# An attention and MoE kernel: sums' rows ahead of loads on the queue, ScalarE's exponentials ahead of its copies

## The chip, the cores and the metric

The kernel runs on one core of a Trainium2 chip. The core has TensorE (PE, with its weight loads as PEld), VectorE (DVE), ScalarE (ACT), GpSimd (POOL) and SyncE (SP), which here issues every DMA. The metric is the device time of one execution in microseconds (us), taken as the median of several runs.

## The reference

Causal attention over 2 batches of 12 heads, 448 positions, 64 elements per head; its output, laid out as 896 rows of 768, goes through two feed-forward blocks. Everything is float32.

```python
scores = np.where(mask, -1e9, scale * q @ k.T)          # mask: above the diagonal
attn = np.exp(scores - scores.max(-1, keepdims=True))
attn = attn / (attn.sum(-1, keepdims=True) + 1e-09)
x = (attn @ v)                                          # as 896 x 768
h = np.maximum(np.maximum(x @ w1, x @ w2), x @ w3)      # 768 x 768 each
x = h @ w_out
r = np.maximum(x @ w_in, 0.0)                           # 768 x 2048
out = (s * (r * r) + b) @ w_out2                        # 2048 x 768
```

## The kernel before, in words

The first fifth of the time is attention, the rest the feed-forward blocks, whose weights come as 56 tiles (`wraw`) that VectorE and ScalarE decode into a high and a low part. Attention works on 12 pairs of heads in 14 software-pipelined steps. The order of all instructions is the order of the code (`manual_schedule`): in step `s` (`step`, L534) four pairs are in work.

- Pair `s` ("new"): TensorE lays the mask into three PSUM tiles and adds the scores to it: A holds query rows 256 to 383 of both heads, B rows 0 to 255, C the last 64 rows of both heads. Scores are products of a high and a low part (`HL`) of q and k. VectorE takes row minima (`minima`; scores are negated), ScalarE the exponentials (`exps`: index 2 is A, 0 and 1 are B, NQ is C), which also give the row sums `su`, seven numbers for each of 128 partitions.
- Pair `s-1` ("old"): VectorE inverts the sums (`inverses`, L444: add 1e-9, take the reciprocal). TensorE transposes the exponentials in four groups (`transposes`); each group is copied out of one of two PSUM tiles `t` to `PT` (`pt_copy`: groups 0 to 2 by ScalarE, group 3 by VectorE). Between groups 1 and 2 stand the product with V of pair `s-2` and the transpose `st` of the inverted sums (`sums`). `spread` (L456) copies `st` to `rows`, writes `rows` to DRAM (`rcd`) by two DMAs and reads it back by two DMAs as a broadcast `rb`, which have to wait for the write.
- Pair `s-2` ("out"): the product with V (`pv`). It runs over four column blocks j; block j needs the V rows from 128j on.
- Pair `s-3`: `pv_out` (L472) multiplies the product in PSUM by `rb` on VectorE (`xf`), which also frees the one PSUM tile `o` for the next `pv`; GpSimd splits the result for the feed-forward blocks.
- Pair `s+2` ("nxt"): VectorE rounds q and k to the high part (`split_hi`), GpSimd takes the low part (`split_lo`) and copies the last rows into the block-diagonal `bd` (`both_tails`). For pair `s+3` GpSimd scales q (`scaled`).

SP issues in the order of the code and stops at a DMA whose wait has not ended. A DMA also waits for the landing of the eighth one before it, whose semaphore it takes over. At the start of a step stand the load of q and k of pair `s+4` (`R`, 448 KB) and some of the 42 loads of V; the table `V_LOADS` says how many stand there and how many between the write `rcd` and the broadcast `rb`. V comes in four groups: pair 0, pair 1, pairs 2 to 5 (first needed by `pv` in step 4) and pairs 6 to 11 (first needed in step 8). Weight tiles are fetched behind `spread`. Steps 12 and 13 have no new scores; TensorE fills them with the first feed-forward products.

Of the kernel before, what the change touches and what calls it, by code (L numbers as in the profile page):

```python
# [14 lines left out]
ALU = mybir.AluOpType  # L15
# [20 lines left out]
    12: ("hi2", "low3"),  # L36
}
V_GROUPS = ((0, 1), (1, 1), (2, 4), (6, 6))
V_LOADS = ((7, 0), (3, 4), (3, 4), (3, 4), (2, 2), (2, 2), (2, 2), (2, 0))
FILL = {12: (3, 5), 13: (0, 4)}  # L40
WARM = 9
BUSY = (9,)
# [7 lines left out]
def kernel(  # L50
# [39 lines left out]
    def sub_lo(eng, lo, full, hi):  # L90
        eng.tensor_tensor(out=lo, in0=full, in1=hi.bitcast(F32), op=ALU.subtract)  # L91
# [122 lines left out]
    def attention():  # L214
        with ExitStack() as c2:
# [36 lines left out]
            def load(p, cuts=((0, S),)):  # L252
                pair[p]["R"] = R = ld.tile([128, 2, S], F32, tag="R", name="R")
                for a, b in cuts:
                    nc.sync.dma_start(out=R[:, :, a:b], in_=qk[p, :, :, a:b])
# [17 lines left out]
            def load_v(n):  # L273
                for _ in range(min(n, len(v_list))):
                    to, of = v_list.pop(0)
                    nc.sync.dma_start(out=to, in_=of)  # L276
# [13 lines left out]
            def scaled(p):  # L290
                q = pair[p]["R"][:, 0, :]
                pool_scaled(q, q, -scale)
# [4 lines left out]

            def split_lo(p):
                HL, R = pair[p]["HL"], pair[p]["R"]
                sub_lo(nc.gpsimd, HL[:, 1:4:2, :], R, HL[:, 0:4:2, :])  # L300

            def split_hi_early(p):
                new_hl(p)
# [16 lines left out]
            def both_tails(p):  # L320
                HL = pair[p]["HL"].bitcast(F32)
                for h in range(2):
                    pool_scaled(bds[p % 3][hs[h], :, hs[h]], HL[hs[h], 0:2, TAIL:S], 1.0)
# [47 lines left out]
            def minima(p, i):  # L371
                e = pair[p]
                src, cols = (at(p, i), slice(2 * i, 2 * i + 2)) if i < NQ else (e["C"][:, 0:S], slice(2 * NQ, 2 * NQ + 1))
                nc.vector.tensor_reduce(  # L374
                    out=e["mx"][:, cols], in_=src, axis=mybir.AxisListType.X, op=ALU.min
                )
# [14 lines left out]
            def exps(p, i):  # L391
                if i == NQ:
                    exponential(p, pair[p]["C"][:, 0:S], L0, S, 2 * NQ, NQ)
                    return
                for h in range(2):
                    exponential(
                        p, at(p, i)[:, h], p_at(h, i, 0), (i + 1) * TQ, 2 * i + h, h * (NQ + 1) + i
                    )
# [44 lines left out]

            def inverses(p):  # L444
                su = pair[p]["su"]
                nc.vector.tensor_tensor(
                    out=su, in0=su, in1=tiny.to_broadcast([128, 7]), op=ALU.add
                )
                nc.vector.reciprocal(out=su, in_=su)

            def sums(p):
                e = pair[p]
# [81 lines left out]
            def step(s):  # L534
                new, old, out, nxt = (
                    p if 0 <= p < n_pairs else None for p in (s, s - 1, s - 2, s + 2)
                )
                if s + 4 < n_pairs:
                    load(s + 4)
                loads = V_LOADS[s] if s < len(V_LOADS) else (0, 0)  # L540
                load_v(loads[0])
                if new is not None:
                    results(new)
                    if new == 0:
# [21 lines left out]
                if new == 1:  # L566
# [2 lines left out]
                    scores_ab(new, 0)  # L569
                    mask_c(new)  # L570
                    scores_c(new)
                if old is not None:
                    inverses(old)
                if new == 0:
                    for i in (0, 1, 2, NQ):
                        minima(new, i)
                elif new is not None:
                    minima(new, 2)
                if new == 1:
                    split_hi(2)  # L580
                    split_lo(2)
                    both_tails(2)
                    for V in vs[2:]:
                        nc.gpsimd.memset(V[D:128, :, :, NQ, :], 0.0)
                if 0 <= s - 3 < n_pairs - 2:
                    pv_out(s - 3)
                if new:
                    for i in (1, 0, NQ):
                        minima(new, i)
                if old is not None:  # L590
                    pt_copy(old, 0, nc.scalar)
                    pt_copy(old, 1, nc.scalar)
                if new:
                    exps(new, 2)
                if new and s + 3 < n_pairs:
                    scaled(s + 3)
                if new and nxt is not None:
                    split_hi(nxt)
                    split_lo(nxt)
                    both_tails(nxt)  # L600
                if s < len(BUSY):
                    keep_busy(BUSY[s])
                if out is not None:
# [7 lines left out]
                    exps(new, 2)  # L611
                if old is not None:
                    sums(old)
                    spread(old, loads[1])
                    transposes(old, 2)
                    transposes(old, 3)
                for _ in asked + [n for n in FETCH if n == s]:
                    fetch_w()
                asked.clear()
                if old is not None:  # L620
                    pt_copy(old, 2, nc.scalar)
                if new is not None:
                    exps(new, NQ)
                decode(MID.get(s, ()))
                if old is not None:
                    pt_copy(old, 3, nc.vector)
# [197 lines left out]
```

## Time and profile before

| | |
|---|---|
| median of 3 runs | 514.69 us (513.52 to 515.76) |
| the profiled execution's own time | 514.35 us |
| its span from first to last instruction | 512.6 us |
| TensorE busy | 499.0 us, 97% |
| VectorE, ScalarE, GpSimd busy | 348.0, 280.5 and 68.8 us |
| GpSimd's last work | before 110 us of the span |
| DMA bytes moved | 58.34 MB |

The busy shares are means over two stages. Up to about 108 us the attention steps follow each other; all four engines and the queue are in use there, and GpSimd only there. Behind that TensorE works without a gap but the last microseconds. A step can be timed by the mask matmul of tile A (L328), which is the first that TensorE does in it: steps 1 to 11 start at 11.09, 17.27, 23.81, 30.95, 39.79, 46.32, 53.40, 60.78, 71.68, 78.67 and 86.24 us.

### The profile page before, as it was taken

The page shows a single profiled execution, that of the slowest core. Times are in us where ns is not written, and L with a number is a line of the kernel's source. Part 1 is how long each engine was busy: PE and PEld are TensorE (multiplying, and loading weights), DVE is VectorE, ACT ScalarE, POOL GpSimd, SP SyncE. Part 2 cuts the span into 40 slices and gives each one's busy share as a digit, 9 for nine tenths or more (in the row PEclk, how much of TensorE's full clock was granted, in tenths as well). Part 3 has the DMA queues.
Part 4 walks back from the last instruction along what each step waited for, and adds up shares of the span by engine and source line. Part 5 has one row for each costly group of instructions (what it writes and reads, how often), then busy time and mean ns, then how long its engine had stood idle before and what let it go on. Part 6 is the DMA issues. An engine that isn't in the chain of part 4 may idle for free.

```text
span 512.6 us, 7545 instructions
## 1 busy us (share of the span) xinstructions
PE 499.0 (97%) x2910; PEld 454.6 (89%) x2910; DVE 348.0 (68%) x522; ACT 280.5 (55%) x517; POOL 68.8 (13%) x93
## 2 busy tenths in 40 slices
PE   8899979999999999999999999999999999999997
PEld 4767757789999999999999999999999999999997
DVE  4788879558476675758767888888888645384401
ACT  5876757644353453535445787878788333352201
POOL 7876664320000000000000000000000000000000
PEclk9999989999999999999999999999999999999999
DMA  6567631423241332433322332233223333081003
GB/s 197 185 180 213 162 107 38 153 68 123 84 159 66 123 88 98 132 116 124 123 85 101 124 123 82 106 124 123 95 90 124 123 125 123 1 293 61 1 0 109
DMA packets 26068, 58.34 MB, mean 114 GB/s; under 512 B 13532, under 2 KB 17456, under 8 KB 26032
## 3 DMA queue, kind: packets, MB, share of 16 engines
q1 hardware_dynamic: 26032, 57.86, 34.8%
q8 instruction: 23, 0.38, 0.3%
q14 instruction: 13, 0.11, 0.1%
HBM read 55.05 MB, written 2.80 MB: 113 GB/s over the span
## 4 chain that ended last, share of the span: by engine, by line
PE 82%; DMA 7%; DVE 4%; SPq 2%; POOL 2%; ACT 2%; issue 1%; POOLq 0%; DVEq 0%; ACTq 0%
PE m L649 57%; PE m L757 23%; DMA v<-in_v_dram 3%; DMA rcd<-rows 2%; DMA R<-in_qk_dram 1%; PE o L429 1%; SPq L276 1%; POOL HL L91 1%; ACT p L386 1%; DVE mx L374 1%; PE t L413 1%; DVE wa L165 1%; SPq L468 1%; DMA rb<-rcd 1%; PE o L433 1%
## 5 line engine op out<-in xcount | busy, mean ns | idle before, releaser
L649 PE MATMUL m<-x,whi 128*128 128x448 f32 x816 | 232.1, 366 | 1.2 <-ACT wr L146 0.8
L649 PEld LDWEIGHTS m<-x,whi 128*128 128x128 f32 x816 | 152.9, 188 | 13.8 <-ACT wr L146 1.2
L649 PE MATMUL m<-x,wlo 128*128 128x448 f32 x408 | 149.0, 365 | 0.0
L757 PE MATMUL m<-whi,g 128*128 128x384 f32 x448 | 113.9, 334 | 0.0
L183 ACT CAST whi<-wa 128x768 fp32r<-128x768 f32 x56 | 46.8, 835 | 66.5 <-PE m L757 42.3
L649 PEld LDWEIGHTS m<-x,wlo 128*128 128x128 f32 x408 | 76.6, 188 | 6.1
L757 PEld LDWEIGHTS m<-whi,g 128*128 128x128 f32 x448 | 80.8, 188 | 0.0
L143 ACT ACTIVATE wa<-wraw 128x768 f32<-128x768 f32 x56 | 50.9, 910 | 53.7 <-DVE wlo L91 51.2
L91 DVE TENSOR_TENSOR wlo<-wa,whi 128x768 fp32r<-128x768 f32 x56 | 53.5, 956 | 38.9 <-ACT whi L183 38.9
L757 PE MATMUL m<-wlo,g 128*128 128x384 f32 x224 | 74.8, 334 | 0.0
L178 DVE CUSTOM_DVE_ANT_0 wa<-wa,wr 128x1536 uint16<-128x1536 uint16 x56 | 53.6, 957 | 1.9
L171 DVE SCALAR_TENSOR_TENSOR wa<-wraw,wa 128x768 int32<-128x768 int32 x56 | 53.5, 955 | 0.0
L146 ACT ACTIVATE wr<-wraw 128x768 int32<-128x768 uint32 x56 | 50.8, 907 | 0.0
L757 PEld LDWEIGHTS m<-wlo,g 128*128 128x128 f32 x224 | 42.0, 188 | 0.0
L656 DVE TENSOR_TENSOR t<-t,m 128x448 f32<-128x448 f32 x24 | 14.9, 621 | 38.7 <-PE m L649 38.7
L649 PE MATMUL m<-h,whi 128*128 128x448 f32 x144 | 40.9, 365 | 0.0
L165 DVE TENSOR_SCALAR wa<-wa 128x768 int32<-128x768 int32 x56 | 34.2, 610 | 1.8
L419 ACT COPY PT<-t 128x512 f32<-128x512 f32 x36 | 20.2, 597 | 22.1 <-PE t L413 22.1
L742 ACT ACTIVATE r<-m 128x448 f32<-128x448 f32 x32 | 17.5, 546 | 22.1 <-PE m L649 22.1
L429 PE MATMUL o<-PT,v 128*64 128x448 f32 (+3 forms) x96 | 24.8, 401 | 4.8 <-DVE xf L477 4.4
L157 DVE TENSOR_SCALAR wa<-wa 128x768 f32<-128x768 f32 x52 | 28.7, 552 | 0.6 <-ACT wa L143 0.6
L649 PEld LDWEIGHTS m<-h,whi 128*128 128x128 f32 x144 | 27.0, 188 | 2.1
(81 smaller groups left out, 566.1 us busy)
## 6 DMA issues: line engine op xcount, KB each, us to landing
wraw<-in_w_dram SPq DMA_DIRECT2D x56, 768.0 KB, 4.3
R<-in_qk_dram SPq DMA_DIRECT2D x11, 448.0 KB, 5.4
rb<-rcd SPq DMA_DIRECT2D x24, 112.0 KB, 2.7
out_dram<-o SPq DMA_DIRECT2D x14, 192.0 KB, 1.9
v<-in_v_dram SPq DMA_DIRECT2D x4, 96.0 KB
v<-in_v_dram SPq DMA_DIRECT2D x2, 168.0 KB, 6.5
v<-in_v_dram SPq DMA_DIRECT2D x6, 48.0 KB, 2.6
v<-in_v_dram SPq DMA_DIRECT2D x2, 144.0 KB, 4.6
```

Of the source, the lines that this page charges most:

```text
L91: eng.tensor_tensor(out=lo, in0=full, in1=hi.bitcast(F32), op=ALU.subtract)
L143: nc.scalar.activation(out=e["f"], in_=e["high"].bitcast(F32), func=ACTF.Abs)
L146: nc.scalar.activation(out=e["r"], in_=e["low"].bitcast(U32), func=ACTF.Copy, scale=2.0 ** -29)
L157: nc.vector.tensor_scalar(out=e["f"], in0=e["f"], scalar1=UNDER, scalar2=OVER, op0=ALU.max, op1=ALU.min)
L165: nc.vector.tensor_scalar(out=a, in0=a, scalar1=3, scalar2=0x3FFFFFF8, op0=ALU.logical_shift_left, op1=ALU.bitwise_and,)
L171: nc.vector.scalar_tensor_tensor(out=e["a"], in0=e["high"], scalar=-0x40000000, in1=e["a"], op0=ALU.bitwise_and, op1=ALU.bitwise_or,)
L178: nc.vector.tensor_tensor(out=e["a"], in0=e["a"], in1=e["r"], op=ALU.add)
L183: nc.scalar.copy(out=e["hi"], in_=e["f"])
L419: copy(out=pair[p]["PT"][:, n * 512:(n + 1) * 512], in_=pair[p]["t", n])
L429: nc.tensor.matmul(o[hs[0], j * TQ:S], V[:, 0, j], PT[:, at:at + m * TQ + D], **flags)
L649: nc.tensor.matmul(p, wt[w][:, ws], cols(act[i], a, b), start=(i == 0 and n == 0), stop=(i == len(act) - 1 and n == 2),)
L757: nc.tensor.matmul(acc[t][:, 0:EH], gt[f][:, a, ts], w[:, ws], start=(f == 0 and n == 0), stop=(f == KG - 1 and n == 2),)
```

## The change

What it does, in the order of a step:

- The load of q and k of pair `s+4` and the loads of V leave the step's start. `load(s+4)` stands behind `spread`, with V loads behind it; a new `V_LOADS` (first number: between write and broadcast; the others: behind) sets how many.
- `inverses` keeps the reciprocal alone and stands behind the minima of A. The add of 1e-9 is done by ScalarE (`guarded`), right behind the last exponentials of the pair, a step earlier.
- From step 2 on ScalarE takes the exponentials of A ahead of the copies of transpose groups 0 and 1.
- The low parts are taken in two instructions of half the size.
- `scaled(s+3)` stands behind the low parts and tails instead of ahead of them; in step 1 the high and low part of pair 3 stand behind `spread`.

```diff
-V_LOADS = ((7, 0), (3, 4), (3, 4), (3, 4), (2, 2), (2, 2), (2, 2), (2, 0))
+V_LOADS = ((0, 7, 7), (2, 3), (2, 3), (2, 2), (2, 2), (2, 2), (2, 1), (2, 1))
...
-                sub_lo(nc.gpsimd, HL[:, 1:4:2, :], R, HL[:, 0:4:2, :])
+                for n in range(2):
+                    sub_lo(nc.gpsimd, HL[:, 2 * n + 1], R[:, n], HL[:, 2 * n])
...
             def inverses(p):
                 su = pair[p]["su"]
-                nc.vector.tensor_tensor(
-                    out=su, in0=su, in1=tiny.to_broadcast([128, 7]), op=ALU.add
-                )
                 nc.vector.reciprocal(out=su, in_=su)
+
+            def guarded(p):
+                su = pair[p]["su"]
+                nc.scalar.activation(out=su, in_=su, func=ACTF.Identity, bias=tiny)
...
-                if s + 4 < n_pairs:
-                    load(s + 4)
                 loads = V_LOADS[s] if s < len(V_LOADS) else (0, 0)
-                load_v(loads[0])
...
-                if old is not None:
-                    inverses(old)
                 if new == 0:
                     for i in (0, 1, 2, NQ):
                         minima(new, i)
                 elif new is not None:
                     minima(new, 2)
+                if old is not None:
+                    inverses(old)
...
+                if new is not None and new > 1:
+                    exps(new, 2)
                 if old is not None:
                     pt_copy(old, 0, nc.scalar)
                     pt_copy(old, 1, nc.scalar)
-                if new:
+                if new == 1:
                     exps(new, 2)
-                if new and s + 3 < n_pairs:
-                    scaled(s + 3)
-                if new and nxt is not None:
+                if nxt is not None and new > 1:
                     split_hi(nxt)
                     split_lo(nxt)
                     both_tails(nxt)
+                if new is not None and new > 1 and s + 3 < n_pairs:
+                    scaled(s + 3)
...
                     sums(old)
-                    spread(old, loads[1])
+                    spread(old, loads[0])
                     transposes(old, 2)
                     transposes(old, 3)
+                if s + 4 < n_pairs:
+                    load(s + 4)
+                load_v(loads[1])
                 for _ in asked + [n for n in FETCH if n == s]:
                     fetch_w()
                 asked.clear()
+                load_v(sum(loads[2:]))
+                if new == 1:
+                    split_hi(nxt)
+                    split_lo(nxt)
+                    both_tails(nxt)
+                    scaled(s + 3)
...
                 if new is not None:
                     exps(new, NQ)
+                    guarded(new)
```

SP's queue around step 3, before: the load of q and k of pair 7 stands first, the write of pair 2's rows after three V loads, the broadcast last (`v_100` is V of pairs 2 to 5; its 64-row pieces are the last that the product of step 4 needs).

```order
L255 DMA R<-in_qk_dram 128x896
L276 DMA v_100<-in_v_dram 32x4x64
L276 DMA v_100<-in_v_dram 80x4x64 x2
L462 DMA rcd<-rows 7x128
L463 DMA rcd<-rows 1x64
L276 DMA v_100<-in_v_dram 48x4x64 x2
L276 DMA v_100<-in_v_dram 64x4x64 x2
L468 DMA rb<-rcd 64x448 x2
```

The same step on SP's queue, now:

```order
L464 DMA rcd<-rows 7x128
L465 DMA rcd<-rows 1x64
L276 DMA v_100<-in_v_dram 48x4x64 x2
L470 DMA rb<-rcd 64x448 x2
L255 DMA R<-in_qk_dram 128x896
L276 DMA v_100<-in_v_dram 64x4x64 x2
L128 DMA wraw<-in_w_dram 128x768
```

The write and the broadcast now stand first; the load of q and k and the last two pieces of V for step 4 have moved behind the broadcast.

ScalarE in step 2, before (PT is the transposed exponentials, `p` the exponentials of the three score tiles, `su` their sums):

```order
L419 COPY PT<-t 128x512 x2
L386 ACTIVATE p_134,su<-A,mx 128x384 x2
L386 ACTIVATE p_134,su<-B,mx 128x128 x2
L386 ACTIVATE p_134,su<-B,mx 128x256 x2
L419 COPY PT<-t 128x512
L386 ACTIVATE p_134,su<-C,mx 128x448
```

ScalarE in step 2, now:

```order
L387 ACTIVATE p_134,su<-A,mx 128x384 x2
L420 COPY PT<-t 128x512 x2
L387 ACTIVATE p_134,su<-B,mx 128x128 x2
L387 ACTIVATE p_134,su<-B,mx 128x256 x2
L420 COPY PT<-t 128x512
L387 ACTIVATE p_134,su<-C,mx 128x448
L451 ACTIVATE su<-su,tiny 128x7
```

A's exponentials have moved ahead of the two copies, and the add of the constant is new at the end.

VectorE at the start of step 3, before:

```order
L446 TENSOR_TENSOR su<-su,tiny 128x7
L449 RECIPROCAL su<-su 128x7
L374 TENSOR_REDUCE mx<-A 128x2
L477 TENSOR_TENSOR xf<-o,rb 128x448
```

VectorE at the start of step 3, now:

```order
L375 TENSOR_REDUCE mx<-A 128x2
L447 RECIPROCAL su<-su 128x7
L479 TENSOR_TENSOR xf<-o,rb 128x448
```

The minima of A no longer stand behind the inverted sums, and the add has left VectorE.

## Rows read from the trace of the kernel before

**Rows 1.** TensorE's waits: who waited for whom, total us, times, longest.

```profile
PE o L429 <- DVE xf L477: 4.4, 4, 2.8
...
PE t L413 <- DVE rows L461: 1.2, 1, 1.2
...
PE B L336 <- ACT p L386: 0.7, 3, 0.3
```

**Rows 2.** Timeline of TensorE, 30 to 72 us: start, duration, operation [idle before].

```profile
30.95 0.28 PE L328 MATMUL A<-tri,identb 128*128 128x128 bf16 x2
...
39.79 0.28 PE L328 MATMUL A<-tri,identb 128*128 128x128 bf16 x2
...
44.94 0.22 PE L429 MATMUL o<-PT,v 128*64 128x64 f32 x1
...
45.18 0.28 PE L454 MATMUL st<-ident,su 128*7 128x128 f32 x1
...
46.32 0.28 PE L328 MATMUL A<-tri,identb 128*128 128x128 bf16 x2
...
60.78 0.28 PE L328 MATMUL A<-tri,identb 128*128 128x128 bf16 x2
...
67.11 0.59 PE L429 MATMUL o<-PT,v 128*64 128x448 f32 x1 [2.77 <-DVE xf L477]
...
71.68 0.28 PE L328 MATMUL A<-tri,identb 128*128 128x128 bf16 x2
```

**Rows 3.** Stretches: length, busy us (instructions) by engine, PE clock, DMA share, GB/s.

```profile
65.00:67.50 2.50, 0.39 (x2) 0.27 (x4) 1.07 (x2) 1.21 (x5) 0.65 (x3) 1.00 0.97 257
67.50:70.00 2.50, 2.50 (x22) 1.87 (x18) 1.98 (x4) 1.72 (x8) 2.42 (x4) 0.56 0.22 48
...
125.00:150.00 25.00, 25.00 (x125) 23.17 (x124) 17.81 (x27) 11.54 (x16) 0.00 (x0) 1.00 0.38 126
```

**Rows 4.** Chain of waits, 0 to 130 us: start, duration, what.

```profile
35.98 2.37 DMA v<-in_v_dram
```

**Rows 5.** Timeline of SP's queue, 52 to 81 us.

```profile
56.81 0.33 SPq L462 DMA_DIRECT2D rcd<-rows  x1
...
62.89 1.09 SPq L468 DMA_DIRECT2D rb<-rcd  x2
...
64.66 1.30 SPq L276 DMA_DIRECT2D v<-in_v_dram  x2
...
78.14 0.27 SPq L462 DMA_DIRECT2D rcd<-rows  x1
...
79.36 1.09 SPq L468 DMA_DIRECT2D rb<-rcd  x2
```

**Rows 6.** Timeline of VectorE in steps 1, 2, 7, 8 and 10.

```profile
15.67 0.86 DVE L296 CAST HL<-R 128x896 fp32r<-128x896 f32 x1
...
22.98 0.28 DVE L461 COPY rows<-st 7x128 f32<-7x128 f32 x1 [1.50 <-PE st L454]
...
54.93 0.95 DVE L446 TENSOR_TENSOR su<-su,tiny 128x7 f32<-128x7 f32 x1 [0.44 <-ACT p L386]
...
66.43 0.62 DVE L477 TENSOR_TENSOR xf<-o,rb 128x448 f32<-128x448 f32 x1 [3.36 <-DMA rb<-rcd]
...
79.51 1.86 DVE L165 TENSOR_SCALAR wa<-wa 128x768 int32<-128x768 int32 x1
```

**Rows 7.** Groups by line and shape, ScalarE to 92 us: count, busy us, mean ns, idle before.

```profile
L419 ACT COPY PT<-t 128x512 f32<-128x512 f32 x32 | 17.9, 596 | 19.4 <-PE t L413 19.4
```

**Rows 8.** The same for GpSimd to 104 us.

```profile
L91 POOL TENSOR_TENSOR HL<-R,HL 128x896 fp32r<-128x896 f32 x11 | 25.8, 2343 | 2.1 <-DVE HL L296 2.0
L91 POOL TENSOR_TENSOR x<-xf,x 128x448 fp32r<-128x448 f32 x11 | 12.5, 1138 | 0.9
```

**Rows 9.** DMA issues of the page: count, KB each, median us to landing.

```profile
R<-in_qk_dram SPq DMA_DIRECT2D x11, 448.0 KB, 5.4
rb<-rcd SPq DMA_DIRECT2D x24, 112.0 KB, 2.7
```

## The prediction, made before the changed kernel was run

> **What bounds the kernel now.** I read the busy shares by stretch first. Behind attention TensorE is busy for the whole of a stretch at full clock [rows 3], so whatever attention saves or loses there comes through to the end unchanged. The change touches attention alone, and it leaves TensorE's own order as it was. So the question is how much TensorE waits in attention, for whom, and which of these waits goes.
>
> The measure is the length of a step from one mask matmul of A to the next. Step 5 takes 46.32 - 39.79 = 6.53 us [rows 2], and no later step with scores is shorter: I take it as what TensorE needs if nothing keeps it waiting. Step 4 takes 39.79 - 30.95 = 8.84 us, step 8 takes 71.68 - 60.78 = 10.90 us [rows 2]. These two hold most of what can be had: 2.31 and 4.37 us. The rest is in TensorE's list of waits [rows 1]: 4.4 us for `xf` in four waits (2.77 of them in step 8 [rows 2], so 1.6 in the other three), 1.2 us once for `rows` in step 1, and 0.7 us in three waits of the mask of B for ScalarE's exponentials.
>
> Step 8 read from its end: the product with V waits 2.77 us for `xf` [rows 2], which waits 3.36 us for the broadcast `rb` [rows 6]. That broadcast is issued at 62.89, 6.08 us after its write at 56.81 [rows 5]; where nothing else is under way the same distance is 79.36 - 78.14 = 1.22 us [rows 5]. So the write stood behind loads, and SP, which waits for it in order, held up everything behind. Around this wait TensorE is busy 0.39 of 2.50 us, and then the granted clock is 0.56 of full, a mixture of 1.2 and 2.4 GHz [rows 3]. That is where the step's other 4.37 - 2.77 = 1.6 us go.
>
> Step 4 waits for V: the last piece is issued at 35.98 and lands 2.37 us later, on the chain [rows 4]. Of the 2.31 us I put 0.24 down to a mask wait and 2.07 to V.
>
> **The change part by part.**
>
> Write and broadcast ahead of the loads. The 6.08 us shrink towards 1.22 [rows 5], and SP is no longer held for long. Step 8's broadcast then lands in time: from `st` of step 6 to the `xf` that uses it are 46.32 - 45.18 = 1.1 us to the next step [rows 2], one step of 6.53, and in step 8 at least the 2.5 us that step 7 needed to the end of its inverted sums (54.93 + 0.95 - 53.40 [rows 6]), 10.1 in all. The way there is about 0.7 us to the write's issue (0.28 for `st` [rows 2], 0.28 for `rows` [rows 6], the rest between them), 1.2 to the broadcast's, 1.1 for its two issues [rows 5] and 2.7 to landing [rows 9], 5.7 us. Even with the old 6.08 us between write and broadcast it would be 10.6, half a us late. So the whole 4.37 us go, the clock's part included: -4.4.
>
> What the loads pay for it. The load of q and k of one pair moves about one step back. Its landing takes 5.4 us under load [rows 9], its user (`scaled`) stands a step later: hidden, with about 1 us to spare, and nothing if GpSimd waits a little, since the low part is used two steps on. V is another matter. The last pieces for step 4 and for step 8 now stand behind the broadcast and the load of q and k of the step before. From `st` in that step: 0.7 us to the write's issue, 1.22 to the broadcast [rows 5], 64.66 - 62.89 = 1.77 for the two broadcast issues and the load of q and k, 0.65 for the first of two V issues (half of 1.30) [rows 5], then 2.37 from issue to landing [rows 4]: 6.7 us. TensorE needs the last V block one step after `st` less 45.18 - 44.94 = 0.24 us [rows 2], so 6.3 us. At best it waits 0.4 us there. At worst the write is held up as at 56.81, 6.08 instead of 1.22 us [rows 5], and it waits 5.3 us. I am nearer to the first end: what stands ahead of the write in step 3 is one load of q and k (448 KB) and three V pieces (192 KB), and at the 257 GB/s of a full stretch [rows 3] that is 2.5 us, of which some 2 pass while they are being issued. Before, the write at 56.81 had a weight tile of 768 KB on top. So about 0.5 us on the best case: 0.9 us of waiting is left in step 4 instead of 2.07, -1.2; and in step 8, where V comes late too once `xf` is in time, +1.0.
>
> A rule of the Trainium skill speaks against this ordering. The row says 1.22 us from the write of the sums to the broadcast on an empty queue [rows 5]. The page "DMA: Bandwidth & Descriptors", section "Anatomy of one DMA", puts the fixed part of a DMA at about 2.0 us, most of it the receipt of the write, longest towards DRAM. By it (it is fitted to another way of issuing) V would come 0.8 us later in both steps and the sum be 1.6 us worse; the row is from this very pair of DMAs, so I stay with it.
>
> Step 1. `rows` no longer stands behind a rounding of 0.86 us [rows 6] whose place is now after it. Of the 1.2 us that the transposes wait for `rows` [rows 1] I take 0.7, since the minima ahead of it stay: -0.7 (0.4 to 0.9).
>
> Step 2. `scaled(4)` now stands behind pair 3's low part and tails, and the rounding of pair 4 waits for it, with `rows` behind it on VectorE. Price from 0, since VectorE had 1.50 us to spare there [rows 6], to 2.3, the length of the low part [rows 8]. Nearer to the first: +0.3.
>
> ScalarE. It idles 19.4 us over 32 copies, always for the transposes [rows 7]; the exponentials of A can stand in just that gap once their minima are there, so that the exponentials of B end earlier and the next step's mask of B no longer waits: -0.7, all of rows 1. The added operation of 128x7 costs less than a copy of 128x512 (0.596 us [rows 7]) and lies in the same gap: 0. Without that gap it would be up to 12 x 0.6 us of ScalarE, still not TensorE's.
>
> VectorE. The add waited 0.44 us for ScalarE and took 0.95 us in step 7 [rows 6], with the minima of A and `xf` behind it. Both go. That pays in the three smaller waits for `xf`: 1.6 us. In step 10 a decoding operation of 1.86 us stands ahead [rows 6] and stays; I take 0.9 of the 1.6.
>
> Low parts in halves: 2 x 1.138 = 2.28 us instead of 2.343 [rows 8]. GpSimd has slack either way: 0.
>
> The sum: -4.4 - 1.2 + 1.0 - 0.7 + 0.3 - 0.7 - 0.9 = -6.6 us. The profiled execution took 514.35 us, 1.75 more than its span and 0.34 less than the median. So 507.75 for a run like it, and 508.1 as a median.
>
> **The rivals.**
>
> V late, slower. If the write keeps standing behind loads in steps 3 and 7 as at 56.81, V is 5.3 us late in both, and after each of these waits, both longer than the 2.77 us of step 8, the clock falls as it did there for 1.6 us. Against the forecast that is 5.3 - 0.9 = 4.4 in step 4, 5.3 - 1.0 = 4.3 in step 8, and 3.2 for the clock: 508.1 + 11.9 = 520.0. For it: step 4 waits for V already, and these pieces alone lose places on the queue. Against it: no weight tile stands ahead of the write in steps 3 and 7. With the clock falling both times it eats the whole gain from a wait w of 2.7 us in each of the two places (2 x (w - 0.95) + 3.2 = 6.6), and is slower by over 0.5% from 4.0 us (the same sum, 9.2).
>
> V late by half. Waits of 2.9 us in each place, as long as that of step 8, with one fall of the clock: 2.0 + 1.9 + 1.6 = 5.5 on top, 513.6. The same evidence, with the queue half as full.
>
> The broadcast is not earlier enough. It still has to wait for its write, and in step 6 a weight tile, a load of q and k and two V pieces stand ahead of that as before. If `xf` in step 8 still waits half of its 2.77 us and the clock still falls, 1.4 + 1.6 = 3.0 us of the gain stay away: 511.1. A late `xf` covers a late V in step 8, so the 1.0 us there may fall away as well: 510.1. Against it: the 4 us of margin worked out above.
>
> **How the numbers follow.** The forecast, 508.1, has 0.58; the broadcast not early enough (510.1 to 511.1) 0.12; V late by half (513.6) 0.17; V late, slower (520.0) 0.13. A difference of 0.5%, 2.6 us, is about what a measurement of this kernel can tell from no change: 512.1 to 517.3 is the same. So faster 0.70, same 0.17, slower 0.13. The forecast's own range goes from 505.0 (all of the 1.6 us of `xf`, 0.9 in step 1, nothing lost in step 2, V only 0.4 late in both places: 0.7 + 0.2 + 0.3 + 1.1 = 2.3 better, and some more where step 5 is not the floor) to 510.5 (each part at half). To leave out no more than 2 in 10 the range goes up to 513.9, past V late by half.
>
> **What would show it.** Steps 6 to 9 at 6.5 to 6.8 us each; the distance from write to broadcast under 3 us in all steps but 2 and 6, and SP idle between; step 1 at about 5.5; no wait of the mask of B for ScalarE; no half clock near 68 us. Right but mis-sized would be waits of TensorE for V in steps 4 and 8 of 0.4 to 2 us. Wrong would be V waits of 3 us and over with the clock at half behind them, or a new wait of VectorE for GpSimd's `scaled`, which would say that the later loads of q and k and not V set the pace.

## The result, and the profile after

The changed kernel took 519.82 us (median of four: three took 519.51 to 519.84, one took 2466.65), the kernel before 514.37 us beside it: a ratio of 1.0101 with a 95% interval of 1.0072 to 1.013. It is slower by 1%. Run once more on another chip it took 520.72 us against 515.52, a ratio of 1.0116 (1.008 to 1.0152); the profile shown here is of that second run. One caution for the medians and ratios further down: on some chips the stage behind the last product with V takes either 408.4 or 414.0 us in the traces, whichever kernel runs, so that both depend on how many of each were among the runs.

So the kernels are compared by **the length of attention** in their traces, from the first mask matmul of A in step 1 to the last product with V. For the kernel before it is 104.15 - 11.09 = 93.06 us, for the changed kernel 112.51 - 12.26 = 100.25 us, 7.2 us more. Each length is that of one profiled execution; the one kernel that was profiled twice, V early in the next section, gave 87.19 and 87.42 us. (The profiled execution of the changed kernel is the longest of its four, 522.71 us, which adds to the difference.)

TensorE's list of waits in the changed kernel (who waited for whom, total us, times, longest), beside [rows 1]:

```profile
PE o L430 <- DMA v<-in_v_dram: 5.5, 1, 5.5
PE o L439 <- DMA v<-in_v_dram: 4.7, 1, 4.7
...
PE o L430 <- DVE xf L479: 0.7, 1, 0.7
PE t L414 <- DVE rows L463: 0.5, 1, 0.5
PE B L337 <- ACT p L387: 0.3, 1, 0.3
```

What was to go has gone: the waits for `xf` fell from 4.4 us to 0.7, those for `rows` from 1.2 to 0.5, those of the mask of B from 0.7 to 0.3. Two new lines stand above them, and together they are 10.2 us. TensorE's timeline says where (start, duration, operation, idle time before):

```profile
43.69 0.48 PE L430 MATMUL o<-PT,v 128*64 128x64 f32 x2 [5.48 <-DMA v<-in_v_dram]
...
77.95 0.47 PE L439 MATMUL o<-PT,v 128*64 128x64 f32 x2 [4.71 <-DMA v<-in_v_dram]
```

The first is the last block of the product in step 4, which is the first product with V of pairs 2 to 5; the second is the same block in step 8, the first product with V of pairs 6 to 11. Around both the clock fell. Stretches of the changed kernel (length, busy us and instructions of TensorE, its weight loads, VectorE, ScalarE and GpSimd, granted clock, DMA share, GB/s):

```profile
38.21:42.98 4.77, 0.00 (x0) 0.00 (x0) 0.00 (x0) 0.00 (x0) 3.70 (x5) 1.00 0.70 183
42.98:49.81 6.83, 6.12 (x37) 5.42 (x38) 3.33 (x7) 2.82 (x7) 0.56 (x1) 0.50 0.72 204
...
77.11:83.94 6.83, 5.99 (x35) 5.29 (x36) 3.86 (x8) 2.08 (x6) 0.60 (x2) 0.50 0.11 37
```

And the one such stretch of the kernel before, behind the wait of 2.77 us in step 8 [rows 2, 3]:

```profile
67.90:71.31 3.41, 3.41 (x26) 2.90 (x23) 2.25 (x5) 1.72 (x8) 3.41 (x3) 0.51 0.19 55
```

0.50 is the lower of the two levels, 1.2 of 2.4 GHz. Eight transposes take 1.71 us at 44.67, within such a stretch, and 0.87 us at 50.45, behind it; so I count half of the busy time as lost: 6.12 / 2 = 3.1 us and 5.99 / 2 = 3.0 us after the change, 3.41 / 2 = 1.7 us before it.

The steps, each from its first mask matmul to that of the next (us; step 11 to the last product with V), with those of the first repaired version of the next section:

| step | 1 | 2 | 3 | 4 | 5 | 6 | 7 | 8 | 9 | 10 | rest |
|---|---|---|---|---|---|---|---|---|---|---|---|
| before | 6.18 | 6.54 | 7.14 | 8.84 | 6.53 | 7.08 | 7.38 | 10.90 | 6.99 | 7.57 | 17.91 |
| changed | 5.40 | 7.03 | 6.53 | 14.95 | 8.14 | 6.54 | 6.54 | 12.84 | 8.18 | 6.71 | 17.39 |
| V early | 5.40 | 7.01 | 6.54 | 7.63 | 6.54 | 8.04 | 6.54 | 8.33 | 7.08 | 6.70 | 17.38 |

Steps 4 and 5 lose 7.7 us together and steps 8 and 9 lose 3.1; all others together gain 3.7. Steps 4 and 5 stand 23.09 - 2 x 6.53 = 10.0 us over the floor: 5.5 of waiting for V, 0.7 for `xf`, 3.1 for the clock, and 0.8 not put down to anything. Steps 8 and 9 stand 8.0 us over it: 4.7, 3.0 and 0.3.

Why V is late there is read from SP's queue. Its timeline through steps 2 and 3 (start, time spent issuing, line, transfer, count):

```profile
23.39 0.48 SPq L128 DMA_DIRECT2D wraw<-in_w_dram  x1
24.16 0.28 SPq L464 DMA_DIRECT2D rcd<-rows  x1
...
30.15 2.01 SPq L470 DMA_DIRECT2D rb<-rcd  x2
32.25 0.58 SPq L255 DMA_DIRECT2D R<-in_qk_dram  x1
32.88 1.41 SPq L276 DMA_DIRECT2D v<-in_v_dram  x3
34.39 0.31 SPq L464 DMA_DIRECT2D rcd<-rows  x1
...
37.10 1.09 SPq L470 DMA_DIRECT2D rb<-rcd  x2
38.28 0.54 SPq L255 DMA_DIRECT2D R<-in_qk_dram  x1
38.87 1.30 SPq L276 DMA_DIRECT2D v<-in_v_dram  x2
```

and through the end of step 7:

```profile
68.50 0.35 SPq L464 DMA_DIRECT2D rcd<-rows  x1
...
72.13 1.10 SPq L470 DMA_DIRECT2D rb<-rcd  x2
...
73.91 0.63 SPq L276 DMA_DIRECT2D v<-in_v_dram  x1
```

Read it backwards from 43.64, where the V piece that the product in step 4 waits for lands. It was issued at 38.87, behind the broadcast of 37.10. That waited 2.71 us for its write of 34.39. And the sums of that write had been in SBUF since 30.67 (VectorE's row: `rows` at 30.39, 0.28 us long): SP was still held by the broadcast of step 2, which waited 5.99 us for a write issued right behind a weight tile (24.16 to 30.15), and then by the loads that were queued behind that broadcast.

### The profile page after: what moved, and what is told of

Same layout as the page of the kernel before. It is cut to its first block, busy times and chain, and to the rows that moved or that the text cites. A ratio compares the mean times of both kernels' runs of the same rounds, so it can differ in the third digit from the quotient of the medians.

```text
span 2464.9 us, 7546 instructions
## 1 busy us (share of the span) xinstructions
PE 2459.3 (100%) x2910; PEld 1833.2 (74%) x2910; DVE 339.7 (14%) x510; ACT 285.4 (12%) x529; POOL 63.6 (3%) x104
## 4 chain that ended last, share of the span: by engine, by line
PE 100%; DVE 0%; ACT 0%; issue 0%; ACTq 0%
PE m L660 65%; PE m L768 17%; PE t L414 5%; PE o L430 3%; PE o L434 2%; PE C L367 2%; PE A L359 2%; PE B L359 2%; PE warm L486 1%; PE B L337 1%; PE o L439 0%; PE st L456 0%; PE A L329 0%; PE C L344 0%; DVE t L667 0%; DVE ones L492 0%
## 5 line engine op out<-in xcount | busy, mean ns | idle before, releaser
L660 PE MATMUL m<-x,whi 128*128 128x448 f32 x816 | 1048.8, 1465 | 0.8 <-DVE t L667 0.8
L660 PEld LDWEIGHTS m<-x,whi 128*128 128x128 f32 x816 | 695.8, 854 | 205.3 <-issue 205.1
L660 PE MATMUL m<-x,wlo 128*128 128x448 f32 x408 | 596.9, 1463 | 0.0
L660 PEld LDWEIGHTS m<-x,wlo 128*128 128x128 f32 x408 | 348.0, 853 | 101.3 <-issue 98.6
L768 PE MATMUL m<-whi,g 128*128 128x384 f32 x448 | 337.2, 889 | 0.0
L768 PEld LDWEIGHTS m<-whi,g 128*128 128x128 f32 x448 | 197.0, 440 | 78.8 <-issue 61.5
L768 PE MATMUL m<-wlo,g 128*128 128x384 f32 x224 | 199.2, 889 | 0.0
L660 PE MATMUL m<-h,whi 128*128 128x448 f32 x144 | 193.4, 1529 | 0.0
L414 PE MATMUL t<-ident,p 128*128 128x128 f32 x192 | 136.9, 1045 | 0.0
L660 PE MATMUL m<-h,wlo 128*128 128x448 f32 x72 | 109.8, 1525 | 0.0
```

What stands on the lines that cost most here:

```text
L414: nc.tensor.transpose(t[:, m * TQ:(m + 1) * TQ], e["P"][:, a:a + TQ], ident)
L660: nc.tensor.matmul(p, wt[w][:, ws], cols(act[i], a, b), start=(i == 0 and n == 0), stop=(i == len(act) - 1 and n == 2),)
L768: nc.tensor.matmul(acc[t][:, 0:EH], gt[f][:, a, ts], w[:, ws], start=(f == 0 and n == 0), stop=(f == KG - 1 and n == 2),)
```

## The experiments

Lengths of attention, for reference: before 93.06, changed 100.25.

**The changed kernel again, and three kernels that part the change in two.** The first is the changed kernel as it was. The second changes V's distribution alone, so that no load of V for steps 4 and 8 is left to steps 3 and 7:

```diff
-V_LOADS = ((0, 7, 7), (2, 3), (2, 3), (2, 2), (2, 2), (2, 2), (2, 1), (2, 1))
+V_LOADS = ((0, 7, 7), (4, 3), (4, 3), (4, 0), (4, 0), (4, 0), (2, 0), (0, 0))
```

The third is the kernel before with the new order on the queue and the new `V_LOADS` (`load(s + 4)` and `load_v` behind `spread`), but with every engine's order as before. The fourth is the changed kernel with the queue's old order and old `V_LOADS`, the engines' new order kept.

> The changed kernel once more, beside the kernel before on the same chip. It took 519.8 us in its first runs, 1.0% longer, at a mean granted clock near 0.987 (before: 0.996). Theory V (the last pieces of V land late): TensorE waits for V in steps 4 and 8, 3 to 5 us each, and the clock falls to half behind each wait; 519 to 520 us. Theory E (the new order on ScalarE and VectorE costs): no wait for V over 2 us, instead waits for copies, sums or exponentials in every step. Theory R (the loads of q and k come late): waits of GpSimd's scaling for R and of TensorE for HL.

> The changed kernel with a V_LOADS that brings V earlier: four pieces between write and broadcast instead of two, so that pairs 2 to 5 are loaded in step 2 and pairs 6 to 11 in step 6. Nothing else is changed. Theory V: the waits for V go and with them the fall of the clock, 506 to 510 us. Theory E and theory R: no change, 519 to 520 us.

> The kernel before with the queue's part alone: loads behind write and broadcast, and the new V_LOADS; the order on the other engines is the old one, the low parts are whole. Theory V: V is as late as with the whole change, 518 to 522 us. Theory E: the queue's part is the gain and the rest the loss, 507 to 511 us. Theory R: 518 to 522 us.

> The changed kernel with the old queue: the loads of q and k and of V stand where they stood before, with the old V_LOADS; ScalarE, VectorE and GpSimd have the new order. Theory V: a small gain, the waits for the mask of B and a part of those for the scaled output go, 511 to 513 us. Theory E: 518 to 522 us. Theory R: 511 to 513 us.

Measured on one chip, the kernel before at 515.52 us: the changed kernel 520.72 us, ratio 1.0116 (1.008 to 1.0152); V early 508.72 us, 0.9879 (0.9844 to 0.9914); the queue alone 520.55 us, 1.0117 (1.0081 to 1.0153); the engines alone 512.43 us, 0.9947 (0.993 to 0.9964). Attention: 100.25, 87.19, 99.11 and 91.44 us. TensorE's waits with V early:

```profile
PE o L430 <- DVE xf L479: 3.3, 3, 1.6
...
PE o L430 <- DMA R<-in_qk_dram: 0.6, 1, 0.6
```

and with the queue's order alone:

```profile
PE o L429 <- DMA v<-in_v_dram: 5.2, 1, 5.2
PE o L438 <- DMA v<-in_v_dram: 3.4, 1, 3.4
```

No wait for V is left in the first, and the new order on the queue brings both waits into the kernel before without anything else of the change. The line for `R` is no cost of the later loads of q and k: it is a wait in step 4 that ends at 34.55, just behind `xf` (33.87, 0.62 us long), which frees the PSUM tile; in a second trace of this kernel the same wait is put down to `xf`. The loss is V's distribution, and the engines' part gains. The 13.1 us of attention between the changed kernel and V early (12.0 us in the medians) decide the sign of the whole change. Theory V's ranges hold for the last three kernels; the first is 0.7 us above its range.

**One V at a time.** The first brings forward V of pairs 2 to 5 and leaves that of pairs 6 to 11 where the change put it. The second keeps the change's numbers but lets V pass the load of q and k behind the broadcast. The third fetches the weight tile of step 1 in step 0, so that none stands ahead of the write in step 2.

```diff
-V_LOADS = ((0, 7, 7), (2, 3), (2, 3), (2, 2), (2, 2), (2, 2), (2, 1), (2, 1))
+V_LOADS = ((0, 7, 7), (4, 3), (4, 3), (0, 0), (2, 2), (2, 2), (2, 1), (2, 1))
```
```diff
+                load_v(loads[1])
                 if s + 4 < n_pairs:
                     load(s + 4)
-                load_v(loads[1])
```
```diff
-FETCH = (0, 1, 3)
+FETCH = (0, 0, 3)
```

> The changed kernel with V of pairs 2 to 5 early (loaded by step 2, as in e1) and V of pairs 6 to 11 where the change has it. If each late V costs by itself (its wait plus its own fall of the clock), the wait of 5.5 us in step 4 and its half clock go and those of step 8 stay: about half of the 12 us between e0 and e1, 513 to 516 us. Rival: what is won in step 4 is waited for again in step 8, since the later loads are paced by the queue and not by TensorE: 517 to 520 us.

> The changed kernel with the V loads behind the broadcast issued ahead of the load of q and k instead of behind it. If the load of q and k (448 KB) ahead of V is a part of the 4.8 and 4.0 us from V's issue to its landing, V lands 1.5 to 2 us earlier in both places, the clock still falls: 516 to 518 us. Rival: the queue position behind q and k does not matter, the time goes from write to broadcast: 520 to 521 us.

> The changed kernel with the second weight tile fetched in step 0 instead of step 1, so that no weight tile stands ahead of step 2's write of the sums, which took 6.0 us to the broadcast in e0. If that tile is what held it, the distance falls to 2 to 3 us, SP reaches step 3's write about 3 us earlier (34.4 us in e0), and the wait for V in step 4 falls from 5.5 to 2 to 3 us; step 8 as in e0: 516 to 518 us. Rival: the other loads hold it, 520 to 521 us.

Medians: 518.67, 520.1 and 519.6 us, the kernel before at 520.09 us; the ratios, 1.0016 (0.9961 to 1.0072), 0.996 (0.9897 to 1.0023) and 1.0085 (1.0032 to 1.0139), carry the scatter of that chip. All three medians lie above the ranges of the first theory, two of them in that of the rival, but the kernel before, too, took 4.6 us more on this chip than on the first; what follows is read from the traces. Attention: 93.24, 94.89 and 94.42 us. The longest waits for V in the first kernel (one), the second (two) and the third (two):

```profile
70.58 0.47 PE L439 MATMUL o<-PT,v 128*64 128x64 f32 x2 [5.09 <-DMA v<-in_v_dram]
```
```profile
40.60 0.33 PE L430 MATMUL o<-PT,v 128*64 128x64 f32 x2 [2.50 <-DMA v<-in_v_dram]
...
73.39 0.33 PE L439 MATMUL o<-PT,v 128*64 128x64 f32 x2 [2.63 <-DMA v<-in_v_dram]
```
```profile
39.05 0.33 PE L430 MATMUL o<-PT,v 128*64 128x64 f32 x2 [3.25 <-DMA v<-in_v_dram]
...
71.93 0.47 PE L439 MATMUL o<-PT,v 128*64 128x64 f32 x2 [4.37 <-DMA v<-in_v_dram]
```

Each V has its own price: with that of step 4 repaired attention is 7.0 us shorter than in the changed kernel, and 6.05 us longer than with both repaired. Passing the load of q and k (448 KB) takes 3.0 and 2.1 us from the two longest waits; in step 4 two waits for other pieces, 0.9 us each, come up in their place, so that 1.2 us of waiting go there and 2.1 in step 8. The third kernel shows the hand-over from step 2 to step 3. Its queue:

```profile
24.30 0.32 SPq L464 DMA_DIRECT2D rcd<-rows  x1
...
27.04 1.09 SPq L470 DMA_DIRECT2D rb<-rcd  x2
...
30.31 0.31 SPq L464 DMA_DIRECT2D rcd<-rows  x1
...
33.41 1.09 SPq L470 DMA_DIRECT2D rb<-rcd  x2
...
35.19 1.58 SPq L276 DMA_DIRECT2D v<-in_v_dram  x2
```

Without the tile ahead of it the write of step 2 is read back 2.74 us later instead of 5.99, SP is free when step 3's sums come, and V leaves 5.9 us behind `st` (29.32 to 35.19) instead of 8.8 (30.08 to 38.87). It is still late: 3.25 us for its first user and 0.54 us for the next.

**The weight tiles on another queue.** The changed kernel, with the weight tiles of attention from step 1 on issued by ScalarE (`nc.scalar.dma_start`) instead of SP; V as the change put it.

> The changed kernel, V where the change put it, with the weight tiles of the attention's steps from 1 on issued from ScalarE's queue. If the tile of the step before is what holds SP and so V, the write of step 2 is no longer 6.0 us ahead of its broadcast, the loads behind it leave about 3 us earlier, and of the waits for V, 5.5 and 4.7 us in the changed kernel, 0 to 2.5 us are left in each; the last product with V then ends at 103 to 107 us instead of 112.51. If the 16 DMA engines are simply full of loads by then, whatever queue they come from, the waits stay at 4 to 5.5 us each and it ends at 111 to 113 us.

518.36 us beside 519.48 (ratio 0.9967, 0.9926 to 1.0008); attention 92.18 us, its last product at 103.93 us. Its end is in the first theory's range, but the two waits went different ways (the last row shows that of step 8):

```profile
42.67 0.47 PE L430 MATMUL o<-PT,v 128*64 128x64 f32 x2 [5.12 <-DMA v<-in_v_dram]
71.92 0.33 PE L439 MATMUL o<-PT,v 128*64 128x64 f32 x2 [1.36 <-DMA v<-in_v_dram]
```

In step 8 4.7 us became 1.4; there the tile leaves at 49.32, 8.7 us ahead of the write of step 6 (58.06), which is read back 1.7 us later. In step 4 almost nothing was won, and the reason is the second theory's. The tile that SP had issued behind V, at 40.21, is now issued by ScalarE at 28.29, since ScalarE doesn't wait for the broadcast; and the write of 30.51 is read back only at 36.07, though no tile stands ahead of it in its own row. Its piece in the chain of waits, the tile's issue, and the stretches between:

```profile
30.51 5.50 DMA rcd<-rows
```
```profile
28.29 0.34 ACTq L128 DMA_DIRECT2D wraw<-in_w_dram  x1
```
```profile
30.00:32.00 2.00, 2.00 (x22) 1.61 (x22) 2.00 (x3) 1.97 (x9) 2.00 (x2) 1.00 0.97 352
32.00:34.00 2.00, 2.00 (x25) 1.84 (x22) 1.98 (x5) 1.71 (x4) 1.03 (x3) 1.00 1.00 322
```

All 16 DMA engines are busy (0.97 and 1.00) with the tile and the loads beside it. With the same loads ahead in SP's row and no tile, in the kernel that fetches it early, the write of step 3 was read back after 3.10 us (30.31 to 33.41). So a small write is held by the bytes that are under way when it is issued, those of the other queue included. The Trainium skill has the shared engines (page "DMA: Bandwidth & Descriptors", section "Queues, rings and completion order"): SP and ScalarE own one row each, with a ring on each of the same 16 engines, and an engine takes the rows in turn. By that the tile would slow down the loads that stand ahead of the write in SP's row, which fits these rows; how the engines divided themselves is not shown.

**Parts that the prediction put at little or nothing**, each undone in the kernel with V early, which ran again as the base: ScalarE's copies ahead of the exponentials of A as before; the low part in one piece; the add of 1e-9 back on VectorE; the last two together.

> e1 with ScalarE's copies ahead of the exponentials of A again, as in the kernel before; the rest of the change stays. By the working of the prediction the exponentials ahead are worth the waits of the mask of B, 0.7 us: 509 to 510 us where e1 is 508.7. Rival: the gap on ScalarE is worth nothing once the sums are off VectorE, 508.7; or the copies matter more, 507 to 508 us.

> The kernel with V brought forward again (the changed kernel with V_LOADS = ((0,7,7),(4,3),(4,3),(4,0),(4,0),(4,0),(2,0),(0,0)), nothing else changed), as the base for the three beside it. Expected 508 to 509 us and a ratio of 0.988 to the kernel before, as in its first run; three waits of TensorE for xf, 3.3 us together, in the steps behind a weight tile, and no wait for V.

> The kernel with V early, with GpSimd's low part in one piece again and the sums' constant still on ScalarE. Compared by the time at which the last product with V ends in the trace: 98.65 us in the base, 100.78 with both parts undone. If the low part carries the 2.1 us (GpSimd's next operation, or a reader of the first half, waits 1.2 us longer), about 100.5; if it is worth nothing, as predicted, 98.6 to 98.9.

> The kernel with V early, with the sums' constant added on VectorE again and the low part in halves. By the same measure: if the addition carries the 2.1 us (it waits on VectorE for ScalarE's last exponentials, with the minima and xf behind it, and rows comes later), 100.5 to 100.8; if it is worth nothing, as predicted, 98.6 to 98.9.

> The base with two parts of the change undone together: the sums' constant is added on VectorE again, with the inverses, and GpSimd takes the low part in one piece. ScalarE's exponentials ahead of its copies stay. The prediction put both parts at nothing. By that 508 to 509 us, the same as the base within 0.3%. If the two parts carry a share of what the engines' part of the change gained (2.6 us in the run with the queue order undone), up to 511 us.

| kernel | median, us | before beside it | ratio (95% interval) | executions under 513 us | attention, us |
|---|---|---|---|---|---|
| V early, again | 509.57 | 516.31 | 0.9856 (0.9793 to 0.9919) | four, 508.78 to 509.81 | 87.42 |
| copies first | 515.48 | 520.09 | 0.9923 (0.9874 to 0.9973) | three, 509.32 to 510.08 | 87.28 |
| low part whole | 515.74 | 519.48 | 0.9902 (0.9857 to 0.9946) | four, 510.44 to 511.77 | 88.93 |
| add on VectorE | 512.17 | 519.48 | 0.986 (0.9775 to 0.9946) | two, 508.67 and 509.22 | 88.63 |
| both of these | 515.11 | 516.31 | 0.9938 (0.9897 to 0.9979) | five, 510.91 to 512.85 | 89.29 |

With the copies first the mask waits are back and the waits for `xf` are shorter, at the same length:

```profile
PE o L430 <- DVE xf L479: 1.7, 3, 0.9
PE B L337 <- ACT p L387: 1.4, 6, 0.3
```

So, in this kernel, the exponentials' place only chooses which of the two TensorE waits for. Of the two parts that were put at nothing the halves are worth 1.5 us in the traces, and the executions under 513 us, too short to hold the longer stage behind attention, bear that out: none of the kernel with the low part whole is as short as any with V early. The add is 1.2 us in its one trace, both together 1.9; but the two executions of its kernel under 513 us are as short as those of V early, so a worth of the add is not shown. The halves' worth is not on GpSimd, which is even longer at it. GpSimd's and then VectorE's timeline with the low part whole:

```profile
22.74 2.10 POOL L91 TENSOR_TENSOR HL<-R,HL 128x896 fp32r<-128x896 f32 x1 [0.81 <-PE o L438]
```
```profile
23.10 2.54 DVE L152 SCALAR_TENSOR_TENSOR wa<-wa,over 128x768 f32<-128x768 f32 x1
```

and in halves:

```profile
22.80 2.97 POOL L91 TENSOR_TENSOR HL<-R,HL 128x448 fp32r<-128x448 f32 x2 [0.81 <-PE st L456]
```
```profile
23.04 1.71 DVE L152 SCALAR_TENSOR_TENSOR wa<-wa,over 128x768 f32<-128x768 f32 x1
```

The same decoding operation takes 2.54 us beside a whole low part, and ends 0.8 us after it (25.64 against 24.84); beside halves it takes 1.71 us, and the halves end later instead: the first takes 1.13 us, the second 1.87. It looks as if VectorE gets in between them. The add shows the same in the kernel that has it on VectorE: 128x7 elements take 0.17 us in one step and 0.75 in the next, where it starts at 40.70 while GpSimd is at its low parts from 38.47 to 41.43, and ends with them, at 41.45:

```profile
32.17 0.17 DVE L447 TENSOR_TENSOR su<-su,tiny 128x7 f32<-128x7 f32 x1
40.70 0.75 DVE L447 TENSOR_TENSOR su<-su,tiny 128x7 f32<-128x7 f32 x1
```
```profile
38.47 2.96 POOL L91 TENSOR_TENSOR HL<-R,HL 128x448 fp32r<-128x448 f32 x2
```

The Trainium skill names a cause that fits these rows (page "SBUF — State Buffer", section "SBUF: two separate sides"): VectorE and GpSimd share a pair of ports as a lock, and an operation of VectorE with two inputs in SBUF waits until the operation of GpSimd that holds it has ended. That this lock is the whole of the halves' 1.5 us wasn't tried by itself.

**Can the rest of the waits go?** With V early three waits for `xf` remain in the list (3.3 us), beside the one in step 4; the two longest, 1.2 and 1.6 us in steps 6 and 8, belong to writes that stand right behind a weight tile (issued at 38.96 and 52.29, read back at 44.32 and 60.16). Two repairs: the tile issued ahead of the load of q and k from step 2 on, and the tiles from step 2 on issued by ScalarE.

> The same with the weight tile that a step of the attention fetches issued right behind the broadcast, ahead of the q and k load, from step 2 on. In the base the tile was issued last in its step and the next write and broadcast stood behind its 768 KB: 38.96 to 44.32 us and 52.29 to 60.16 us, and xf came 1.6 us late. If the place of the tile in the row is what matters, it leaves 0.6 us earlier (the issue of the q and k load), the write behind it the same, and of the 3.3 us of xf waits 1 to 1.8 us go: 506.8 to 508 us. If the queue is simply full in these steps, so that whatever stands ahead the write comes as late, no change: 508 to 509 us.

> The same with the weight tiles of the attention's steps from 2 on issued from ScalarE's queue, so that the write and the broadcast of SP's queue don't stand behind them in one row. If it is the row on the queue that holds the write, the 3.3 us of xf waits go and 4 issues of about 0.45 us on ScalarE are added, which has 0.6 to 0.8 us of idle time in a step: 505.5 to 507.5 us. If it is the 16 DMA engines that are shared, the write and broadcast land as late as before and the waits stay: 508 to 509.5 us, or more by what ScalarE's issues delay.

510.49 us (ratio 0.9845, 0.9778 to 0.9913) and 508.6 us (0.9818, 0.9765 to 0.9872), beside 509.57 for the base; attention 86.46 and 85.71 us against 87.42. The order of the three shows in the traces, in the medians it doesn't, and both medians are above the ranges expected. Against the base's two traces moving the tile by one place gains 0.7 to 1.0 us: the waits for `xf` fall to 1.3 us, but transposes wait 1.9 us for copies, which they didn't before. Another queue gains 1.5 to 1.7: the wait in step 8 is gone, and two of 1.96 and 1.18 us remain in steps 4 and 6. The first is a wait for the broadcast that SP issues at 29.22; ScalarE issues a tile right beside it, at 29.76. V early with the tiles on ScalarE's queue is the shortest attention measured, 7.35 us less than before the change, and 1.8% less time.

## Why the prediction was wrong, point by point

- **The step that failed is the path of V** to steps 4 and 8. I wrote 6.7 us from `st` to the landing, with 0.5 more for loads, against 6.3 that were there. Its four pieces, from the rows above (`st` starts at 30.08 and 66.24 in the changed kernel, at 29.32 in the kernel without a tile ahead of step 2's write):

| | `st` to the write | write to broadcast | to V's issue | issue to landing | sum |
|---|---|---|---|---|---|
| predicted | 0.7 | 1.22 + 0.5 | 1.77 | 0.65 + 2.37 | 7.2 |
| changed, step 3 | 4.31 | 2.71 | 1.77 | 4.77 | 13.6 |
| changed, step 7 | 2.26 | 3.63 | 1.78 | 3.99 | 11.7 |
| no tile in step 2, step 3 | 0.99 | 3.10 | 1.78 | 3.86 | 9.7 |

  In step 3 the largest miss is the first column. I looked for a weight tile in the step of the write alone ("no weight tile stands ahead of the write in steps 3 and 7") and found none. One stood ahead of the write of the step before, and since SP waits for each broadcast in order, the delay of step 2's broadcast was passed on to step 3's write. I had known of steps 2 and 6 that their writes stand behind a tile, and didn't follow SP out of them. The trace of the kernel before had this in its own step 3. There `st` starts at 29.74, and SP's queue goes

```profile
29.35 1.87 SPq L468 DMA_DIRECT2D rb<-rcd  x2
...
33.40 0.31 SPq L462 DMA_DIRECT2D rcd<-rows  x1
...
36.70 1.20 SPq L468 DMA_DIRECT2D rb<-rcd  x2
```

  The broadcast of step 2 held SP, so the write left 3.66 us behind `st`, and with a load of q and k and three V pieces ahead of it, as now, it was read back 3.30 us later: nearer rows than the 0.7 and 1.22 us that I took. The misses in the second and the last column are of one kind: the rows for 1.22 and 2.37 us come from places where the DMA engines had little to do (a share of 0.01 and 0.33), and here they were at 0.81 (step 7's landing: 0.64). The bound at the far end, 6.08 us from write to broadcast, makes 11.6 us in all, near the 13.6 and 11.7 measured, but the time was lost in other columns. Waits of over 3 us with the clock at half behind them are what the prediction itself named as the sign of being wrong.
- **The rival "V late, slower" at 520.0 us**, given 0.13, is what happened, in place and outcome: waits of 5.5 and 4.7 us where it said 5.3 each, and the clock at half behind both. Its working holds in part only: it put the whole delay between write and broadcast, at 6.08 us, where 2.71 and 3.63 were measured. So its total of 520.0 against 519.82 measured is in part luck. It sized the fall of the clock at 1.6 us each, which is right for the step it was read from (1.7), but behind these waits the half clock lasted 6.83 us, not 3.41, and took 3.1 and 3.0 us. All other steps together gained 3.7 us, some 1.7 more than forecast, which made up for part of that.
- Step 8's late broadcast, -4.4: right that it goes; in the changed kernel `xf` of step 8 waits 0.25 us for `rb`, whose write of step 6 is read back 5.0 us later (60.33 to 65.36), and steps 6 and 7 run at 6.54 us. It is not safe, though: with V early that write, right behind a weight tile, is read back 7.9 us later (52.29 to 60.16), and 1.6 of the 2.8 us of waiting are back (step 8 takes 8.33 us). That is the rival "not earlier enough", with the place that it named.
- Step 1, -0.7: 5.40 instead of 6.18, -0.8. Right.
- Step 2, +0.3: +0.5. The size was right, the cause not: neither VectorE nor GpSimd is waited for; 0.33 us of it is the mask of B waiting for ScalarE.
- The waits of the mask of B, -0.7, and of `xf` in steps 7, 9 and 10, -0.9: the steps without V waits (3, 6, 7 and 10) are 2.9 us shorter, at 6.5 to 6.7 us, as the last part of the prediction asked for. But the cause given for the first, exponentials ahead of the copies, is worth nothing by itself in the kernel with V early: undone, attention is as long as with it (87.28 and 87.42 us).
- The halves, 0: 1.5 us in the kernel with V early. I priced them on GpSimd and looked for slack there; in the rows shown what they save is VectorE's time beside GpSimd. The add on ScalarE, 0: 1.2 us in one trace, none in the times, so this term stays open.
- The sum: with V in time attention is 93.06 - 87.19 = 5.9 us shorter, where -6.6 was forecast. That they are near is partly luck. Step 4 gained the 1.2 us forecast, but step 8 gained 2.6 instead of 3.4, step 6 lost 1.0, and the other steps gained 3.1 instead of 2.0.
- The rule of the Trainium skill on the fixed part of a DMA (page "DMA: Bandwidth & Descriptors", section "Anatomy of one DMA"), by which the sum would be 1.6 us worse, pointed the right way but doesn't tell the size: from write to broadcast the rows have 2.71 and 3.63 us here and 1.22 on the empty queue, so a constant doesn't cover them.

## What to carry to other kernels

When a transfer goes behind another one on a queue, follow the issuing engine through the steps ahead as well: an engine that waits in order hands a delay of one step to the first transfer of the next. Price a small round trip through DRAM from a place in the trace with the same loads under way, not from an empty queue, and count the loads of other queues too. Ask of every load that a reorder moves back when its first user needs it, and move those with the nearest user ahead in the same edit; here that alone turned 1% slower into 1.2% faster. Price an operation that is cut or moved also on the engine that works beside it.

## What the runs showed of the hardware that I had not expected

- The half clock came in two lengths, 6.83 us behind waits of 5.48, 4.71, 5.09 and 4.37 us, and 3.41 us behind waits of 2.77 and 3.25 us. The length of the wait does not settle it: with V ahead of the load of q and k a wait of 2.50 us, with waits of 0.9 us on either side, had 6.83 us of half clock (40.9 to 47.7), and with the queue's order alone the wait of 3.4 us in step 8 had none (granted clock 1.00 from 68 to 80 us). The rows of the kernel with the early tile, behind 3.25 and 4.37 us, and of that with V of step 4 alone early, behind 5.09 us:

```profile
39.45:42.86 3.41, 2.94 (x15) 2.48 (x15) 1.55 (x3) 1.23 (x4) 0.21 (x1) 0.50 0.45 180
70.17:77.00 6.83, 5.07 (x31) 4.48 (x33) 2.94 (x5) 1.51 (x4) 1.26 (x4) 0.50 0.21 66
```
```profile
67.81:74.64 6.83, 4.07 (x21) 3.48 (x23) 2.28 (x4) 1.51 (x4) 2.16 (x4) 0.50 0.27 83
```

- With a weight tile of 768 KB just ahead, a write of 3.7 KB was read back about as late when the tile came from ScalarE's queue (30.51 to 36.07 us) as when it came from SP's own (24.16 to 30.15 us). Without it the same writes took 3.10 and 2.74 us (30.31 to 33.41 and 24.30 to 27.04).
- Cutting a GpSimd operation of 2.1 us in two pieces, whose pieces take 2.97 us together, shortened attention by 1.5 us; in the step shown VectorE's operation beside it fell from 2.54 to 1.71 us.
